# Spreading 1 / sum over a head's rows: products of 128 rows and 128 columns in place of 4 or 5 rows and 64 columns

## Chip, cores and metric

The kernel runs on one core of one Trainium2 chip. The metric is the device time of one execution in microseconds (us); of several executions the median counts.

## What is computed

Three stages follow each other, for a batch of 4 sequences of 576 tokens. The first is attention with 8 heads of 64 channels, in which each query row keeps only its 32 largest scores; the change stands here. The second is a gate (a causal convolution of 5 taps and a sigmoid) and two 512x512 products; the third mixes channels and tokens with cosines and sines.

```python
scores = scale * np.matmul(q, k.transpose(0, 1, 3, 2))
kth = np.partition(scores, -top_k, axis=-1)[..., -top_k:-top_k + 1]
scores = np.where(scores >= kth, scores, -1000000000.0)
scores = scores - np.max(scores, axis=-1, keepdims=True)
attn = np.exp(scores)
attn = attn / (np.sum(attn, axis=-1, keepdims=True) + 1e-09)
attn_out = np.matmul(attn, v)
...
x = gate(attn_out) * (attn_out @ w_val) @ w_out
...
theta = x @ w_theta
y = w_tok_r @ (x * cos(theta)) + w_tok_i @ (x * sin(theta))
u = x + y
out = u + np.maximum(u @ w_ch, 0.0)
```

## The kernel before

Attention works on pairs of heads (u, 16 of them), each cut into two **parts** by query tokens: x = 0 holds tokens 0 to 255, x = 1 holds tokens 256 to 575. There are 32 parts. A part is a run of tiles of 128 query rows by 576 keys: for each of the two heads (j) two tiles of 128 tokens (m), and in x = 1 one more tile that holds the last 64 tokens of both heads, one head's in its upper and the other's in its lower half. So a part has n = 4 or 5 tiles, and each has 128 sums of exponentials, one per partition.

The loop at the end of the kernel takes one tile a step, and in each step calls the pieces of several tiles in a written order (`STEP`, `SOON`): the score products (`scores_pe`, L536 and L537, into a PSUM bank for 256 keys and one for 320), their copy out by ScalarE (L550), the search for the 32nd largest value on VectorE and GpSimd (L572 to L599), the exponential (L193), mask and sum (L652), four transposes of the masked tile (L665) and one of its last 64 keys (L669), and the copies of these out (L684, L673). Between the steps `work` issues products of the later stages (L507, L805, L1107), so that TensorE has something to do while VectorE searches; that filling ends with the attention at about 736 us, and what is left of the last sequence runs alone.

Products that are small and need a little PSUM wait in the list `extras` and are put into the unused columns of a score bank: `scores_pe` issues the score products of 256 keys, then what fits beside them, then those of 320 keys, then what fits beside these. ScalarE copies both out later, in the order in which they were issued.

When a part's last tile is masked, `close` (a generator that the loop advances) does for it:

- L709 and L710: rs = 1 / (sums + 1e-9), 128 partitions by n columns, on GpSimd and VectorE.
- `rows` (L714, L717): TensorE transposes rs into n rows of 128, and ScalarE copies them into the SBUF tile rT.
- `columns(m)` for m = 0 and 1 (L731, L734, L738): TensorE spreads the row of head j over the 64 partitions of head j, and ScalarE copies the result into rb, 128 channels by 128 tokens (for m = 1 of x = 1 also the last 64 tokens). The stationary operand of such a product is one column of the identity matrix, read 64 times: with it, 64 output rows are each a copy of one row of rT.
- L758: the product of attention and v, px, in float32, two heads in two halves of the partitions.
- L776: VectorE multiplies px by rb into xT, which the gate and the next product read.

The two heads of `columns(m)` are two products: one writes PSUM partitions 0 to 63, the other 64 to 127. So each part has two **sets** of spreading products, 64 sets in all, and the first of a part (m = 0) stands behind L669, the second (m = 1) behind the score products of 320 keys. A float32 product shows as two MATMUL records in the trace (a transpose shows as one).

Of the kernel before, what the change touches and what calls it, by code (L numbers as in the profile page):

```python
# [11 lines left out]
F32 = mybir.dt.float32  # L12
# [78 lines left out]
def mixer(ctx, tc, qT, kT, vt, w_val, conv_t, w_out, w_theta, w_tok, w_ch, out, flag):  # L91
    nc = tc.nc
    safe = flag is None
    P = 128
# [20 lines left out]
    cp = ctx.enter_context(tc.tile_pool(name="cp", bufs=1))  # L115
    io = ctx.enter_context(tc.tile_pool(name="io", bufs=1))
    sp = ctx.enter_context(tc.tile_pool(name="sp", bufs=1))
    wk = ctx.enter_context(tc.tile_pool(name="wk", bufs=1))
# [44 lines left out]
    ident = cp.tile([P, P], F32, name="ident")  # L163
# [8 lines left out]
    nc.gpsimd.memset(trig_bias[64:], 0.0)  # L172
    half_pi = cp.tile([P, 1], F32, name="half_pi")
    nc.gpsimd.memset(half_pi, math.pi / 2)
    magic = cp.tile([P, 1], F32, name="magic")
    nc.gpsimd.memset(magic, MAGIC)

# [13 lines left out]
    def tabled(out, src, func, **more):  # L191

        ins = nc.scalar.activation(out, src, func, **more).ins  # L193
        table = func == AF.Sin
        if (not table) in last and TABLED:
            tc.add_manual_dep(ins, last[not table].name, mybir.DependencyInfo(
                mybir.DependencyClass.NoSync, mybir.DependencyReason.DATA), reason="one table at a time")
        last[table] = ins
# [489 lines left out]
    def diagonal(hp):  # L688

        if not diagonals:  # L690
            all_of = ml.tile([P, 2 * NC * ROOM[1]], F32, tag="room1", name="diagonals")
            diagonals["all"] = all_of[:, : NP * KW * P].rearrange("p (u k w) -> p u k w", u=NP, k=KW)
        if hp not in diagonals:
            diagonals[hp] = diagonals["all"][:, hp]
            nc.gpsimd.tensor_tensor(diagonals[hp], ident.unsqueeze(1).broadcast_to([P, KW, P]),
                                    W["conv"][:, hp, :].unsqueeze(2).broadcast_to([P, KW, P]), ALU.mult)
        return diagonals[hp]

    def close(part):

        u, x = part["u"], part["x"]
        b, hp = divmod(u, NP)
        lo, hi = COLS[x]
        w = hi - lo
        n = 4 + x
        rs = wk.tile([P, 5], F32, tag="rs", name=f"rs_{u}_{x}", bufs=2)
        rT = wk.tile([5, P], F32, tag="rT", name=f"rT_{u}_{x}")
        rb = wk.tile([P, S - CUT], F32, tag="rb", name=f"rb_{u}_{x}")
        nc.gpsimd.tensor_scalar(rs[:, :n], part["sums"][:, :n], 1e-9, None, ALU.add)  # L709
        nc.vector.reciprocal(rs[:, :n], rs[:, :n])  # L710
        done = set()

        def rows(spare):
            nc.tensor.transpose(spare[:n, :P], rs[:, :n], ident)  # L714

            def f():
                nc.scalar.copy(rT[:n], spare[:n, :P])  # L717
                done.add("rows")
            return f

        def row(k):
            return ident[:n, k : k + 1].broadcast_to([n, 64])

        def columns(m):


            def on_pe(spare):
                c = P + REM * (m * x)
                for j in range(2):
                    r = slice(64 * j, 64 * j + 64)  # L730
                    nc.tensor.matmul(spare[r, :P], row(2 * j + m), rT[:n], start=True, stop=True,  # L731
                                     skip_group_check=True)
                    if c > P:
                        nc.tensor.matmul(spare[r, P:c], row(4), rT[:n, r], start=True, stop=True,  # L734
                                         skip_group_check=True)

                def f():
                    nc.scalar.copy(rb[:, m * P : m * P + c], spare[:, :c])  # L738
                    done.add(m)
                return f  # L740
            return on_pe

        extras.append((P, rows))
        yield
        yield
        asked = "rows" in done
        if asked:
            extras.extend((P + REM * (x * m), columns(m)) for m in range(2))
        yield
        if x == 0:  # L750
            drain(("val", (u - 5) // NP))
        v, pT = part["v"], part["pT"]
        owed[0] -= 8.3 * w
        px = ps_m.tile([P, w], F32, tag="m", name=f"px_{u}_{x}")
        for c in range(NF + 1):
            for j in range(2):
                r, k = (slice(0, P), j * NF + c) if c < NF else (slice(REM * j, REM * j + REM), 2 * NF)
                nc.tensor.matmul(px[64 * j : 64 * j + 64, :], v[r, c, 64 * j : 64 * j + 64], pT[r, k, :],  # L758
                                 start=(c == 0), stop=(c == NF), skip_group_check=True)
        if x == 0:  # L760
            xt = sp.tile([P, PAD + S], F32, tag="xT", name=f"xT_{u}", bufs=5)
            nc.gpsimd.memset(xt[:, :PAD], 0.0)
            xT.setdefault(b, []).append(xt)
        xt = xT[b][hp]
        yield
        while "rows" not in done:
            yield
            yield
        if not asked:
            extras.extend((P + REM * (x * m), columns(m)) for m in range(2))  # L770
        yield
        yield
        while 1 not in done:
            yield
            yield
        nc.vector.tensor_tensor(xt[:, PAD + lo : PAD + hi], px, rb[:, :w], ALU.mult)  # L776
        there.add((u, x))
        split = b in SPLIT
        if not split and x == 0:
            return  # L780
        if split and x:
            g = gate[b][hp]
        else:
            drain(("gate", (u - GB) // NP))
            g = sp.tile([P, S], F32, tag="gp", name=f"gp_{u}", bufs=GB)
            gate.setdefault(b, []).append(g)
        if not split:
            lo = 0
        g = g[:, lo:hi]
        cw = W["conv"]  # L790
        if hp == NP - 1:
            jobs.append(front(b, (x,) if split else (0, 1)))
            if x:
                jobs.append(back(b))
        yield
        yield
        while lacking["conv"]:
            yield
            yield
        taps = [xt[:, k + lo : k + hi] for k in range(KW)]  # L800
        if split:
            owed[0] -= 1.675 * KW * (hi - lo)
            ps = ps_m.tile([P, hi - lo], F32, tag="m", name=f"pconv_{u}_{x}")
            for k in range(KW):
                nc.tensor.matmul(ps, diagonal(hp)[:, k, :], taps[k], start=(k == 0), stop=(k == KW - 1))  # L805
            yield
            yield
            tabled(g, ps, AF.Tanh, scale=0.5)
            ready.add((u, x))
            return  # L810
        nc.scalar.activation(g, taps[0], AF.Copy, scale=cw[:, hp, 0:1])
        for k in CT:
            ct = wk.tile([P, S], F32, tag="ct", name=f"ct_{u}_{x}_{k}")[:, : g.shape[1]]
            nc.scalar.activation(ct, taps[k], AF.Copy, scale=cw[:, hp, k : k + 1])
            nc.gpsimd.tensor_tensor(g, g, ct, ALU.add)
            yield
            yield
        if not CT:
            yield
            yield  # L820
        rest = [k for k in range(1, KW) if k not in CT]
        for k in rest:
            nc.vector.scalar_tensor_tensor(g, taps[k], cw[:, hp, k : k + 1], g, ALU.mult, ALU.add)
            if k == rest[1] and len(rest) > 2 or k == rest[-1]:
                yield
                yield
        tabled(g, g, AF.Tanh, scale=0.5)
        ready.add((u, x))
# [355 lines left out]
    for b in range(B):  # L1184
        late = b == B - 1
        f = 1.275 if b in THREE else 1.675
# [19 lines left out]
    def drain(key):  # L1206

        n = 0
        while key[1] >= 0 and key not in done:
            n += 1  # L1210
            assert n < 1000, (key, [(j.gi_frame.f_code.co_name, j.gi_frame.f_lineno, j.gi_frame.f_locals.get('b')) for j in jobs], sorted(map(str, done))[-40:], len(later), len(mid))
            run_mid()
            now, later[:] = list(later), []
            run(now)
            work(DRAIN)
# [24 lines left out]
    for k, part in enumerate(order):  # L1240
        i0 = part["tiles"][0].i
        u, x = part["u"], part["x"]
# [5 lines left out]
        elif split or x == 0:  # L1248
            when = (i0 - 7, i0 - 5, i0 - 5, i0 - 4, i0 - 3) if split or i0 and order[k - 1]["x"] and order[k - 1]["u"] // NP in SPLIT else (i0 - 9, i0 - 8, i0 - 7, i0 - 6, i0 - 3)
            a = (u, x if split else None)  # L1250
            for step, do in zip(when, (load_heads, split_high, split_low, *(
                    lambda u, x, j=j: double(u, j, x) for j in range(2)))):
# [37 lines left out]
    def begin_close(i):  # L1290
        e = seq[i]
        if e is e.part["tiles"][-1]:
            chains.append(close(e.part))
# [103 lines left out]
```

## Time and profile before

| | |
|---|---|
| median of 3 runs | 849.69 us (846.92 to 850.99) |
| the profiled execution, its own time | 849.38 us |
| its span, first to last instruction | 847.3 us |
| mean granted TensorE clock | 0.964 of full speed |
| TensorE busy | 754.7 us |
| VectorE busy | 679.4 us |
| ScalarE busy | 640.3 us |
| GpSimd busy | 438.5 us |

In the views, PE is TensorE's product and PEld its load of the stationary operand (the two overlap), DVE is VectorE, ACT ScalarE, POOL GpSimd, SP the queue of SyncE. L731 is line 731 of the kernel. "out<-in" names tiles; a shape such as 4*64 4x128 is a stationary operand of 4 rows and 64 columns and a moving operand of 4 rows and 128 columns. The chain of waits is followed back from the last instruction: at each step to what released it, or to the instruction before it on its engine; a piece of it lasts until the next piece begins. Time that an engine is idle and that "issue" ended is time in which it waited for no semaphore that the profile shows.

### The profile page before, as it was taken

To read this page: it belongs to the slowest core of one execution; us is meant where nothing else is said; L and a number is where in the kernel's file an instruction comes from. 1 tells how busy PE (TensorE), PEld (TensorE's weight loads), DVE (VectorE), ACT (ScalarE), POOL (GpSimd) and SP (SyncE) were. 2 spreads that over 40 slices of the span, in tenths; PEclk is the share of its full clock that TensorE was granted. 3 is DMA by queue.
4 is the path that set the end of the run, shared out by engine and by line. 5 is a ranking of instruction groups with operands and counts; after the bars stand their busy time and mean duration, and the time that the engine had idled before them with its cause. 6 is when DMAs were issued, how large, how long until landed. Compare 5 with 4: busy or idle time off the path is not lost.

```text
span 847.3 us, 16018 instructions
## 1 busy us (share of the span) xinstructions
PE 754.7 (89%) x4606; PEld 577.5 (68%) x4606; DVE 679.4 (80%) x2786; ACT 640.3 (76%) x1573; POOL 438.5 (52%) x575
## 2 busy tenths in 40 slices
PE   4478999969898899899699989999999899999995
PEld 3345667535655666677587666768897666798895
DVE  6999999879977888899889879989998686353521
ACT  6688898889778777889689887789987784336511
POOL 4876665545544545457667725537796143004600
PEclk9997799979999899999899999999999999999998
DMA  6566665634440243337455543234664300061002
GB/s 171 140 167 189 163 171 161 176 90 127 117 107 15 58 144 82 94 77 240 112 171 168 151 136 83 44 83 100 184 176 122 100 1 15 1 211 45 2 1 61
DMA packets 73602, 94.37 MB, mean 111 GB/s; under 512 B 13728, under 2 KB 37152, under 8 KB 73504
## 3 DMA queue, kind: packets, MB, share of 16 engines
q1 hardware_dynamic: 73184, 92.82, 40.3%
q8 instruction: 39, 0.64, 0.3%
q14 instruction: 59, 0.48, 0.2%
q10 hardware_dynamic: 320, 0.43, 0.2%
HBM read 49.96 MB, written 13.11 MB: 74 GB/s over the span
## 4 chain that ended last, share of the span: by engine, by line
PE 48%; DVE 27%; ACT 11%; POOL 6%; issue 4%; DMA 3%; SPq 1%; ACTq 0%; POOLq 0%
PE py L1107 8%; PE px L758 7%; DVE cand L572 6%; PE pval L507 5%; DVE thrs L599 4%; PE px2t L507 4%; PE pth L507 4%; PE ph L507 3%; PE pt L665 3%; DVE s L652 3%; PE py L1126 3%; PE ps L536 3%; POOL y L593 2%; DVE cand L578 2%; PE ps L537 2%
## 5 line engine op out<-in xcount | busy, mean ns | idle before, releaser
L593 POOL TENSOR_TENSOR y<-s,n 128x576 f32<-128x576 f32 x144 | 190.6, 1324 | 164.8 <-DVE thrs L599 118.6
L572 DVE MAX8 cand<-s 128x8 f32<-128x96 f32 x864 | 210.2, 244 | 1.4 <-ACT s L550 1.4
L652 DVE SCALAR_TENSOR_TENSOR s<-s,thrs,e 128x576 f32<-128x576 f32 x144 | 139.4, 968 | 9.7 <-ACT e L193 9.7
L585 ACT ACTIVATE n<-s,tops 128x576 bf16<-128x576 f32 x144 | 112.0, 778 | 39.6 <-POOL y L593 18.7
L550 ACT ACTIVATE s<-ps 128x256 f32<-128x256 f32 (+1 forms) x288 | 103.7, 406 | 32.9 <-PE ps L731 15.8
L665 PE MATMUL pt<-ident,s 128*128 128x128 f32 x576 | 96.2, 288 | 26.7 <-ACT pT L684 12.6
L1107 PE MATMUL py<-w_tok,z 128*128 128x256 f32 (+1 forms) x432 | 116.8, 410 | 3.4 <-DVE z L966 3.4
L599 DVE MAX8 thrs<-y 128x8 f32<-128x584 f32 x144 | 109.3, 759 | 6.8 <-POOL y L594 6.4
L758 PE MATMUL px<-pT,v 128*64 128x256 f32 (+3 forms) x640 | 106.7, 432 | 9.0 <-ACT pT L684 8.8
L193 ACT ACTIVATE e<-s,least 128x576 f32<-128x576 f32 x144 | 110.7, 769 | 0.5 <-DVE s L652 0.4
L665 PEld LDWEIGHTS pt<-ident,s 128*128 128x128 f32 x576 | 68.8, 145 | 55.6 <-ACT pT L684 22.4
L536 PE MATMUL ps<-kh_None,q 128*128 128x256 f32 x240 | 92.0, 390 | 4.1 <-ACT s L550 2.2
L684 ACT COPY pT<-pt 128x512 f32<-128x512 f32 x128 | 73.1, 571 | 28.5 <-PE pt L665 15.4
L1107 PEld LDWEIGHTS py<-w_tok,z 128*128 128x128 f32 x432 | 77.8, 191 | 24.0 <-DVE z L966 5.0
L758 PEld LDWEIGHTS px<-pT,v 128*64 128x64 f32 (+1 forms) x640 | 43.6, 140 | 57.6 <-issue 26.5
L576 DVE MAX8 tops<-cand 128x8 f32<-128x48 f32 x432 | 82.7, 191 | 0.1
L537 PE MATMUL ps<-kl_None,q 128*128 128x256 f32 x240 | 71.4, 300 | 0.0
L536 PEld LDWEIGHTS ps<-kh_None,q 128*128 128x128 f32 x240 | 46.4, 193 | 21.1 <-ACT s L550 6.1
L536 PE MATMUL ps<-kh,q 128*128 128x256 f32 (+1 forms) x80 | 37.5, 475 | 20.3 <-ACT s L550 8.6
L578 DVE MATCH_REPLACE8 cand<-tops,cand 128x48 f32<-128x48 f32 x288 | 55.1, 191 | 0.0
L673 ACT COPY pT<-ps 64x128 f32<-64x128 f32 (+1 forms) x160 | 39.3, 245 | 12.6 <-PE ps L669 5.8
L537 PEld LDWEIGHTS ps<-kl_None,q 128*128 128x128 f32 x240 | 47.0, 196 | 2.5 <-issue 0.9
(209 smaller groups left out, 1693.4 us busy)
## 6 DMA issues: line engine op xcount, KB each, us to landing
kh_None<-kh_None SPq DMA_DIRECT2D x48, 144.0 KB, 2.6
kl_None<-kl_None SPq DMA_DIRECT2D x48, 144.0 KB, 2.7
v<-in_vt_dram SPq DMA_DIRECT2D x20, 256.0 KB, 3.5
out_dram<-x2T SPq DMA_DIRECT2D x16, 256.0 KB, 3.2
w<-ch SPq DMA_DIRECT2D x16, 256.0 KB, 4.3
w<-theta SPq DMA_DIRECT2D x16, 256.0 KB, 5.4
raw_hi<-in_w_tok_dram SPq DMA_DIRECT2D x14, 256.0 KB, 4.1
kh<-kh SPq DMA_DIRECT2D x24, 144.0 KB, 2.6
```

The source lines that it names most:

```text
L193: ins = nc.scalar.activation(out, src, func, **more).ins
L507: nc.tensor.matmul(ps[o : o + n], x, y, start=(i + k == 0), stop=(i == last and k == len(ways) - 1), skip_group_check=(n < P))
L536: nc.tensor.matmul(bank[:, :w], q2, kh[:, lo:hi], start=(j == js[0]), stop=False)
L537: nc.tensor.matmul(bank[:, :w], q2, kl[:, lo:hi], start=False, stop=(j == js[-1]))
L572: nc.vector.max(d["cand"][:, k, 8 * x : 8 * x + 8], s_tiles[i][:, x * SUB : (x + 1) * SUB])
L585: nc.scalar.activation(n, s_tiles[i], AF.Sign, bias=d["tops"][:, k, KC - 1 : KC], scale=-(1.0 + 2.0 ** -22), accum_out=acc)
L593: nc.gpsimd.tensor_tensor(y[:, :S], s_tiles[i], d.pop(("n", k)), ALU.mult)
L599: nc.vector.max(thrs[:, N - 1 - i : N - 1 - i + NK], d.pop(("y", k)))
L652: nc.vector.scalar_tensor_tensor(p, p, thr(i), e.exp, ALU.is_ge, ALU.mult, accum_out=part["sums"][:, e.slot : e.slot + 1])
L665: nc.tensor.transpose(e.pt[:, c, :], p[:, c * P : (c + 1) * P], ident)
L758: nc.tensor.matmul(px[64 * j : 64 * j + 64, :], v[r, c, 64 * j : 64 * j + 64], pT[r, k, :], start=(c == 0), stop=(c == NF), skip_group_che ...
L1107: nc.tensor.matmul(ps, z[:, m * P : (m + 1) * P], W["tok"][:, w, lo:hi], start=(i + k == 0), stop=(i == NF))
```

## The change

Seven setup instructions on GpSimd are added per copy of the program (the second copy, for unusual inputs, is not run): `spread` holds six blocks of 64 columns and a seventh, filled with identity columns 0, 2, 1, 3, nothing, 4, nothing. Two neighbouring blocks make one constant of 128 rows and 128 columns: it copies one row of rT to output partitions 0 to 63 and another to 64 to 127. `rT` becomes one tile of 128 rows, cleared once, of which each part overwrites the first n. `columns(m)` then issues one product for both heads; for the last 64 tokens it issues two, which are added in PSUM, each with one zero block.

```diff
@@ setup @@
     half_pi = cp.tile([P, 1], F32, name="half_pi")
     nc.gpsimd.memset(half_pi, math.pi / 2)
+    spread = cp.tile([P, 7, 64], F32, name="spread")
+    nc.gpsimd.memset(spread, 0.0)
+    for i, k in enumerate((0, 2, 1, 3, None, 4)):
+        if k is not None:
+            nc.gpsimd.tensor_copy(spread[:, i, :], ident[:, k : k + 1].broadcast_to([P, 64]))
+    rT = cp.tile([P, P], F32, name="rT")
+    nc.gpsimd.memset(rT, 0.0)
@@ close @@
         rs = wk.tile([P, 5], F32, tag="rs", name=f"rs_{u}_{x}", bufs=2)
-        rT = wk.tile([5, P], F32, tag="rT", name=f"rT_{u}_{x}")
...
-        def row(k):
-            return ident[:n, k : k + 1].broadcast_to([n, 64])
+        def rows_of(i):
+            return spread[:, i : i + 2, :].rearrange("p a w -> p (a w)")
...
                 c = P + REM * (m * x)
-                for j in range(2):
-                    r = slice(64 * j, 64 * j + 64)
-                    nc.tensor.matmul(spare[r, :P], row(2 * j + m), rT[:n], start=True, stop=True,
-                                     skip_group_check=True)
-                    if c > P:
-                        nc.tensor.matmul(spare[r, P:c], row(4), rT[:n, r], start=True, stop=True,
-                                         skip_group_check=True)
+                nc.tensor.matmul(spare[:, :P], rows_of(2 * m), rT, start=True, stop=True,
+                                 skip_group_check=True)
+                for j in range(2 if c > P else 0):
+                    nc.tensor.matmul(spare[:, P:c], rows_of(5 - j), rT[:, 64 * j : 64 * j + 64],
+                                     start=(j == 0), stop=(j == 1), skip_group_check=True)
```

What stands on TensorE in the step of a part with x = 1, before the change (ps is the score bank, kh and kl the keys in two halves, s the masked tile whose last keys L669 transposes):

```order
L537 MATMUL ps_0_1869<-kl_3_1_1738,q_87 128x256
L669 MATMUL ps_0_1869<-ident,s_1270 64x128
L731 MATMUL ps_0_1869<-rT_1_1695,ident 64x128 x2
L536 MATMUL ps_256_1875<-kh_3_1_1737,q_87 128x320
L537 MATMUL ps_256_1875<-kl_3_1_1738,q_87 128x320
L731 MATMUL ps_256_1875<-rT_1_1695,ident 64x128
L734 MATMUL ps_256_1875<-rT_1_1695,ident 64x64
L731 MATMUL ps_256_1875<-rT_1_1695,ident 64x128
L734 MATMUL ps_256_1875<-rT_1_1695,ident 64x64
L665 MATMUL pt_1917<-ident,s_1325 128x128 x4
```

The same step with the change, in which lines stand 7 further down:

```order
L676 MATMUL ps_0_1865<-ident,s_1272 64x128
L735 MATMUL ps_0_1865<-rT,spread 128x128
L543 MATMUL ps_256_1870<-kh_3_1_1733,q_87 128x320
L544 MATMUL ps_256_1870<-kl_3_1_1734,q_87 128x320
L735 MATMUL ps_256_1870<-rT,spread 128x128
L738 MATMUL ps_256_1870<-rT,spread 128x64 x2
L672 MATMUL pt_1911<-ident,s_1325 128x128 x4
```

The new products stand in the places of the old ones. A part with x = 0 has the same step without the products of 64 columns (L734 before, L738 now). The order on VectorE, ScalarE and SyncE is the same in both programs; on TensorE beside this a handful of neighbouring products change places, and on GpSimd the setup grows.

## Rows read from the trace of the kernel before

**Rows 1.** The page: TensorE's busy time; shares of the chain of waits by engine.
```profile
PE 754.7 (89%) x4606; PEld 577.5 (68%) x4606; DVE 679.4 (80%) x2786; ACT 640.3 (76%) x1573; POOL 438.5 (52%) x575
...
PE 48%; DVE 27%; ACT 11%; POOL 6%; issue 4%; DMA 3%; SPq 1%; ACTq 0%; POOLq 0%
```

**Rows 2.** Stretches: us, busy PE, PEld, DVE, ACT, POOL, granted clock, DMA share, GB/s.
```profile
60.00:100.00 40.00, 32.81 (x172) 22.24 (x171) 39.69 (x177) 33.98 (x93) 25.26 (x38) 0.80 0.71 190
...
512.00:562.00 50.00, 50.00 (x294) 36.36 (x290) 44.59 (x208) 38.13 (x95) 25.65 (x34) 1.00 0.35 83
```

**Rows 3.** Records that read rT: duration min/median/max in ns, first and last start.
```profile
L731 PE MATMUL ps<-rT,ident x256: 267/292/472, 61.3 to 735.4; 4*64 4x128 f32 x64, 5*64 5x128 f32 x64
...
L734 PE MATMUL ps<-rT,ident x64: 214/216/217, 139.8 to 735.6; 5*64 5x64 f32 x64
```

**Rows 4.** Chain of waits, 517 to 521.3 us: start us, us, what.
```profile
517.29 0.11 PE ps L669
517.40 0.36 PE ps L731 x4
517.76 0.35 PE ps L536
518.11 0.15 PE ps L537
518.25 0.36 PE ps L731 x4
518.62 0.59 PE pt L665 x4
...
520.74 0.11 PE ps L669
520.84 0.11 PE ps L714
520.95 0.15 PE ps L536
521.10 0.15 PE ps L537
```

**Rows 5.** Waits of TensorE's weight loads: us in total, times, longest us.
```profile
PEld px L758 <- issue: 26.5, 81, 1.0
...
PEld ps L731 <- issue: 11.7, 59, 0.3
```

**Rows 6.** Chain of waits, 137.9 to 141 us: a second set of x = 1.
```profile
139.59 0.37 PE ps L731 x4
139.96 0.12 PE ps L734 x4
140.07 0.59 PE pt L665 x4
```

**Rows 7.** Chain of waits, 691.5 to 703.5 us: two sets back to back.
```profile
692.35 0.58 PE ps L731 x8
692.93 0.20 PE ps L714
693.13 0.44 PE pt L665 x4
...
702.12 0.63 PE ps L731 x8
702.75 0.12 PE ps L734 x2
```

**Rows 8.** Chain of waits: the first and the last set that lies on it.
```profile
97.70 0.62 PE ps L731 x4
...
735.05 0.63 PE ps L731 x8
```

**Rows 9.** Timeline of GpSimd around the end of the setup.
```profile
1.95 0.30 POOL masks.py:199 TENSOR_SCALAR_AFFINE_SELECT ident<-ident 128x128 f32<-128x128 f32 x1
12.44 0.73 POOL L291 TENSOR_TENSOR q<-raw,q 64x256 fp32r<-64x256 f32 x1 [10.18 <-ACT q L289]
```

## The prediction

> **What bounds the kernel now.** I read the page first. TensorE is busy 89% of the span, and the chain that ended last lies 48% on it and 27% on VectorE [rows 1]. So no engine bounds the whole: what a change on TensorE is worth depends on the stretch. The stretches show it [rows 2]: between 60 and 100 us VectorE is busy 39.69 of 40 us and TensorE 32.81, so there VectorE sets the pace; between 512 and 562 us TensorE is busy all 50 us and VectorE 44.59. The reader is to see that TensorE time is worth its full price in stretches of the second kind, and something between nothing and that in the first.
>
> Then I read the lines that the diff touches. L731 has 256 records, four for each of the 64 sets, and L734 has 64, in the 16 second sets of x = 1 [rows 3]. Their busy time is small; what they cost is in the chain, where one step with a set and one without stand three microseconds apart [rows 4]. Without a set, L669, L714, L536 and L537 follow each other by 0.11, 0.11, 0.15 and 0.15 us. With a set, L669 is again 0.11, but L731 holds the chain for 0.36, the L536 behind it for 0.35 instead of 0.15, and the L665 behind the second set for 0.59 instead of the 0.44 that four transposes take behind other transposes or L714 [rows 7]. Weight loads show where it goes [rows 5]: before L731 the load is idle 11.7 us in 59 times, 0.20 us each, with no semaphore to wait for, and before L758 26.5 us in 81 times. L714 is no entry of that kind, though it too reads what another engine has just made, and writes a few columns of the same bank. What L731 and L758 share and L714, L669 and L536 don't is that they write one half of the output partitions each. I conclude that TensorE empties itself when it goes from whole products to halves, and again when it goes back.
>
> The Trainium skill says the same ("TensorEngine Tiling (Array Packing)", Key Properties): changing the tiling mode, not just the tile, drains the engine. The trace agrees as far as it goes: 0.20 us at the way in [rows 5], and at the way out 0.35 against 0.15 [rows 4].
>
> The four records of a set take 0.36 us of chain with some 0.15 to 0.2 of idle in it, though single-file records take 0.11 each, or 0.44 for four. So the two halves run side by side. That is what the change gives up.
>
> **The change part by part.**
>
> *First sets (m = 0).* The new form is one product of whole rows and columns, two records of 128 columns. The trace has no float32 product of just that shape; nearest are L714 and L669, 0.11 us a record [rows 4], so 0.22. The set and the L536 behind it go from 0.36 + 0.35 to 0.22 + 0.15: **0.34 us less**. If emptying stayed, it would be 0 (0.36 + 0.35 again, since a pair side by side takes as long as one whole product); that is the low end.
>
> *Second sets of x = 0.* From 0.36 + 0.59 [rows 4] to 0.22 + 0.44 [rows 7]: **0.29 us less**.
>
> *Second sets of x = 1.* Before, L731, L734 and L665 hold 0.37 + 0.12 + 0.59 = 1.08 us [rows 6]. Now there is the product of 0.22, and two of 64 moving columns for the last tokens, four records. Each streams half as many columns as L714's but must load a stationary operand of 128 columns, which the trace never shows apart from a 128-column stream: between 0.05 (half of 0.11) and 0.11 us, so 0.22 to 0.44 together. With 0.44 for L665 it makes 0.88 to 1.10 us: 0.20 less to 0.02 more. I take **0**, near the upper end, since the only transposes with a stationary operand of 128 columns here, L665's, take 0.11 each.
>
> *The four last parts* have no score products left, and their two sets stand back to back. At 692 us the sets and L714 hold 0.58 + 0.20 [rows 7]; four records and L714 make 5 x 0.11 = 0.55: 0.23 less, twice. At 702 us it is 0.63 + 0.12 + 0.59 [rows 7, 6] against 8 x 0.11 + 0.44 = 1.32: 0.02 less, twice. Together **0.5 us**.
>
> *Setup.* Seven small instructions on GpSimd, none larger than the 0.30 us of the selection in the identity, so at most 2.1 us. GpSimd is idle 10.18 us right behind that selection, until ScalarE has made q [rows 9], and the first use is at 61 us [rows 3]. Nothing is on the path; without that cover it would be 2.1 us, once.
>
> *The rest.* rT was one buffer before and is one now, so ScalarE's copy into it waits for the same readers as before. ScalarE copies the same shapes to rb. The order of VectorE, ScalarE and SyncE is unchanged. Sets get shorter for those who wait behind them as well: ScalarE copies the scores out when the bank's last product is done.
>
> **The sum.** Following the chain through the trace, 32 of the 64 sets lie on it, the first at 97.70 us and the last at 735.05 us [rows 8]; at the others the chain is on another engine or a transfer. The 32 are 12 first sets, 8 second sets of x = 0, 4 second sets of x = 1, and the 8 of the last four parts: 12 x 0.34 + 8 x 0.29 + 0 + 0.5 = 4.1 + 2.3 + 0.5 = **6.9 us**. The profiled execution took 849.4 us (its span is 847.3), 0.3 under the median of 849.7, so the sum gives 842.5.
>
> **The rivals.**
>
> *Every set counts.* The chain is one path of many, and a wait for VectorE is often a wait for scores that TensorE gave late. All sets: 28 x 0.34 + 14 x 0.29 + 0.5 = 14.1 us, 835.3 us; with the low price for the last columns (14 x 0.2 + 0.4 = 3.2 more) 832. For it: TensorE holds 48% of the chain [rows 1]. Against it: between 60 and 100 us VectorE is idle 0.3 of 40 us [rows 2], so it can hardly be served sooner.
>
> *The time is freed and waits again.* The freed time goes into the next wait for VectorE or ScalarE, except where TensorE alone sets the pace: 512 to 562 us [rows 2] with 3 first sets and 2 second sets of x = 0, and the last four parts. That leaves 3 x 0.34 + 2 x 0.29 + 0.5 = 2.1 us: 847.3. For it: outside such stretches the engines are busy to similar shares [rows 1]. Against: the chain already leaves out the stretches where others lead.
>
> *Emptying stays, pairs are lost (slower).* If the idle time belongs to something that the new form keeps, such as reading rT just after ScalarE wrote it, then the sets gain nothing, and the products for the last 64 tokens, which ran side by side, go in single file. Before they add 0.13 us to a set (0.37 + 0.12 against 0.36) [rows 4, 6], now 0.22 to 0.44: 0.09 to 0.31 more. With 6 on the chain that is 0.5 to 1.9 us, with all 16 up to 5: 850 to 854.4, likeliest 851. It decides if the weight load behind L669 still starts 0.3 us late. Against it: L714, which reads rs just written, starts 0.11 behind L669 [rows 4].
>
> The Trainium skill has the rule that this rival rests on ("TensorE: Matmul & The Clock Gate", Part 3): products of fewer than 128 columns, put into different column groups, run at the same time, so it recommends the form that is taken out here. The trace shows that they do run side by side; by that rule alone the change could only lose, some 851 us.
>
> *The clock.* It is granted at 0.80 of full speed between 60 and 100 us [rows 2], so part of the stretch ran at the lower of the two levels. Whether whole products and less idle time move such falls, the trace can't say; either sign, a few us, and it widens the range.
>
> **How the numbers follow.** About 0.5% (4.2 us) is what a measurement of this kernel can tell from no change. The chain's sum, 839 to 845, has 0.53; every set counts, 832 to 839, 0.2; freed time waits again, 845 to 849, 0.22; slower than before 0.05, of which little passes 854. Faster by over 0.5% (under 845.4) is the first two and a bit of the third: 0.76; within 0.5% 0.21; slower 0.03. The range of 8 in 10 runs from 835 to 847.5.
>
> **What would show it right or wrong.** Right: behind L669 the new product starts within 0.12 us, with no idle weight load that "issue" ended; it holds the chain for 0.22, and the L536 behind it for about 0.15. The last-column products are two pairs of records, 0.05 to 0.11 each. The waits of L758 stay at 26 us, since its halves stay. The time from 736 us to the end stays as it is and only moves forward. Wrong: if these steps shrink so and the end does not move by 4 us or more, then the chain overstated TensorE, and waits for VectorE's s, cand or thrs have grown in its place. If the steps do not shrink, halves were not the reason for the idle time. If the time falls by over 12 us, the sets off the chain counted.

## The result, and the profile after

The median went from 849.61 us to 840.25 us (4 executions each): ratio 0.9895, 95% interval 0.9869 to 0.9921. Measured again later, beside two further kernels and more executions of before, the ratio was 0.9916 (0.9902 to 0.9931). By the two ratios the change takes 7 to 9 us off; 842.5 had been forecast, in a range of 835 to 847.5.

The page of the changed kernel, to be held against [rows 1]: busy time by engine, and the shares of the chain of waits.

```profile
PE 737.7 (88%) x4478; PEld 581.3 (69%) x4478; DVE 677.9 (81%) x2786; ACT 639.6 (76%) x1573; POOL 441.4 (53%) x582
...
PE 39%; DVE 28%; ACT 15%; POOL 6%; issue 5%; DMA 4%; SPq 1%; ACTq 0%; POOLq 0%
```

TensorE lost 128 records, and its share of the chain fell from 48% to 39%; ScalarE took 4 of the 9 points. Lines stand 4, 6 or 7 further down than before: L731 is L735, L734 is L738, L758 is L762; L710 is L716, L714 is L720; L669 is L676, L536 is L543, L537 is L544, L665 is L672.

The records that read rT in the changed kernel (columns as in [rows 3]): 128 and 64, with stationary operands of 128 rows and columns.

```profile
L735 PE MATMUL ps<-rT,spread x128: 270/273/275, 61.0 to 726.7; 128*128 128x128 f32 x128
...
L738 PE MATMUL ps<-rT,spread x64: 222/275/275, 139.6 to 727.1; 128*128 128x64 f32 x64
```

The chain of the changed kernel from 512.8 to 517.5 us, the same step as in [rows 4] (start us, us, what):

```profile
513.17 0.11 PE ps L676
513.28 0.22 PE ps L735 x2
513.51 0.15 PE ps L543
513.65 0.14 PE ps L544
513.80 0.22 PE ps L735 x2
514.02 0.44 PE pt L672 x4
```

A set holds the chain for 0.22 us where it held it for 0.36, the product behind the first set for 0.15 where it was 0.35, the four transposes behind the second for 0.44 where they were 0.59. That is what had been worked out, to the hundredth.

The chain of the changed kernel at a second set of x = 1, from 646 to 648 us:

```profile
646.82 0.22 PE ps L735 x2
647.04 0.39 PE ps L738 x4
647.43 0.44 PE pt L672 x4
```

Together 1.05 us, against 1.08 before [rows 6]: 0.03 less. A record of the last tokens takes 0.10 us, though it streams half as many columns as the one ahead of it. Two of the four last parts, in the chain from 684 to 697 us:

```profile
684.29 0.45 PE ps L735 x4
684.73 0.11 PE ps L720
...
693.83 0.45 PE ps L735 x4
694.28 0.39 PE ps L738 x4
694.67 0.44 PE pt L672 x4
```

0.56 against 0.78, and 1.28 against 1.34 [rows 7, 6]: 0.22 and 0.06 less, where 0.23 and 0.02 had been forecast. And the waits of TensorE's weight loads, to be held against [rows 5]:

```profile
PEld pt L672 <- ACT pT L691: 26.4, 21, 6.6
PEld px L762 <- issue: 26.0, 80, 0.5
PEld ps L543 <- ACT s L557: 23.5, 35, 2.3
...
PEld pth L514 <- issue: 6.2, 24, 0.5
```

The 11.7 us of idle loads before the spreading products are gone from the list, and those of L762, which still writes halves, stay. What grew are the waits for ScalarE: for pT 22.4 us before, for s 18.9. A part of the freed time waits there. GpSimd's longer setup went where it was expected (its timeline, changed kernel):

```profile
1.66 0.48 POOL L176 MEMSET spread<- 128x448 f32 x1
...
2.55 0.95 POOL L179 COPY spread<-ident 128x64 f32<-128x64 f32 x5
...
12.30 0.74 POOL L298 TENSOR_TENSOR q<-raw,q 64x256 fp32r<-64x256 f32 x1 [8.59 <-ACT q L296]
```

It ends at 3.5 us, and 8.6 us of the idle time of [rows 9] are left behind it. One of the seven instructions, the clearing of spread, takes 0.48 us, where none had been put over 0.30; with the idle time behind it that costs nothing.

Where the time was gained is read from one instruction of each part, the reciprocal of VectorE (L710 before, L716 after). The table says by how many us it starts sooner than in the trace of before (a minus: later), worked out from the starts in both traces; after_again is a second trace of the changed kernel, and the last two columns belong to experiments below.

| part, start before (us) | changed kernel | after_again | on_chain | off_chain |
|---|---|---|---|---|
| 1st, 49.4 | 0.1 | 0.2 | 0.2 | 0.2 |
| 4th, 101.6 | -0.9 | -0.9 | 0.6 | -0.9 |
| 8th, 200.5 | 0.2 | 0.2 | 1.7 | 0.1 |
| 12th, 294.8 | 0.9 | 0.9 | 3.1 | 0.3 |
| 16th, 377.8 | 3.0 | 2.9 | 3.7 | 0.7 |
| 20th, 465.9 | 4.1 | 4.1 | 4.1 | 0.7 |
| 24th, 552.2 | 5.0 | 5.1 | 5.1 | 0.8 |
| 28th, 634.6 | 7.1 | 6.5 | 4.8 | 1.3 |
| 32nd, 721.3 | 8.3 | 7.8 | 7.2 | 1.3 |

Up to 200 us nothing is gained, and at the 4th part the changed kernel is even 0.9 us late. Then it wins about a microsecond for every two or four parts, and next to nothing more from 736 us to the end (the span is 8.5 us shorter).

### The profile page after: what moved, and what is told of

Same layout as the page of the kernel before. It is cut to its first block, busy times and chain, and to the rows that moved or that the text cites. A ratio compares the mean times of both kernels' runs of the same rounds, so it can differ in the third digit from the quotient of the medians.

```text
span 838.8 us, 15738 instructions
## 1 busy us (share of the span) xinstructions
PE 737.7 (88%) x4478; PEld 581.3 (69%) x4478; DVE 677.9 (81%) x2786; ACT 639.6 (76%) x1573; POOL 441.4 (53%) x582
## 4 chain that ended last, share of the span: by engine, by line
PE 39%; DVE 28%; ACT 15%; POOL 6%; issue 5%; DMA 4%; SPq 1%; ACTq 0%; POOLq 0%
PE py L1111 7%; DVE cand L579 6%; PE px L762 6%; DVE thrs L606 4%; PE pth L514 4%; PE ph L514 3%; DVE s L659 3%; PE px2t L514 3%; PE pval L514 3%; PE py L1130 3%; ACT n L592 3%; PE pt L672 3%; DVE cand L585 2%; ACT e L200 2%; DVE tops L583 2%
## 5 line engine op out<-in xcount | busy, mean ns | idle before, releaser
L659 DVE SCALAR_TENSOR_TENSOR s<-s,thrs,e 128x576 f32<-128x576 f32 x144 | 137.2, 953 | 9.7 <-ACT e L200 9.7
L672 PE MATMUL pt<-ident,s 128*128 128x128 f32 x576 | 95.3, 287 | 29.5 <-ACT pT L691 16.6
L762 PE MATMUL px<-pT,v 128*64 128x256 f32 (+3 forms) x640 | 104.2, 425 | 10.3 <-ACT pT L691 10.3
L672 PEld LDWEIGHTS pt<-ident,s 128*128 128x128 f32 x576 | 69.5, 146 | 56.9 <-ACT pT L691 26.4
L543 PE MATMUL ps<-kh_None,q 128*128 128x256 f32 x240 | 91.2, 387 | 5.0 <-ACT s L557 2.5
L762 PEld LDWEIGHTS px<-pT,v 128*64 128x64 f32 (+1 forms) x640 | 43.1, 137 | 57.0 <-issue 26.0
L544 PE MATMUL ps<-kl_None,q 128*128 128x256 f32 x240 | 71.2, 300 | 0.0
L543 PEld LDWEIGHTS ps<-kh_None,q 128*128 128x128 f32 x240 | 46.3, 193 | 19.4 <-ACT s L557 7.7
L543 PE MATMUL ps<-kh,q 128*128 128x256 f32 (+1 forms) x80 | 35.5, 451 | 22.9 <-ACT s L557 10.0
L544 PEld LDWEIGHTS ps<-kl_None,q 128*128 128x128 f32 x240 | 46.7, 195 | 2.3 <-issue 0.9
```

What stands on the lines that cost most here:

```text
L543: nc.tensor.matmul(bank[:, :w], q2, kh[:, lo:hi], start=(j == js[0]), stop=False)
L544: nc.tensor.matmul(bank[:, :w], q2, kl[:, lo:hi], start=False, stop=(j == js[-1]))
L659: nc.vector.scalar_tensor_tensor(p, p, thr(i), e.exp, ALU.is_ge, ALU.mult, accum_out=part["sums"][:, e.slot : e.slot + 1])
L672: nc.tensor.transpose(e.pt[:, c, :], p[:, c * P : (c + 1) * P], ident)
```

## Experiments

Two questions were open. The prediction took it that TensorE empties itself between products of all output partitions and products of one half. The old form was narrow in two ways, though, few rows and half the columns, and the trace of before had shown neither alone. And it took it that only the sets on the chain count.

**Rows or columns.** few_rows keeps the change's 128 columns, with 4 or 5 rows:

```diff
-                nc.tensor.matmul(spare[:, :P], rows_of(2 * m), rT, start=True, stop=True,
+                nc.tensor.matmul(spare[:, :P], rows_of(2 * m)[:n], rT[:n], start=True, stop=True,
...
-                    nc.tensor.matmul(spare[:, P:c], rows_of(5 - j), rT[:, 64 * j : 64 * j + 64],
+                    nc.tensor.matmul(spare[:, P:c], rows_of(5 - j)[:n], rT[:n, 64 * j : 64 * j + 64],
```

> The change's products of 128 columns, but with only the 4 or 5 rows that carry data (rows of spread and of rT cut to n). Theory A, TensorE empties itself between products that write all output partitions and products that write one half of them: no idle weight load before the spreading products, first sets hold the chain for 0.22 us as after the change, time 840 us (838 to 842). Rival B, it empties because only 4 or 5 of 128 rows are used: the idle 0.20 us before the set and the 0.20 us behind it are back, 847 to 850 us.

halves keeps all 128 rows, with two products of 64 columns:

```diff
-                nc.tensor.matmul(spare[:, :P], rows_of(2 * m), rT, start=True, stop=True,
-                                 skip_group_check=True)
...
+                for j in range(2):
+                    r = slice(64 * j, 64 * j + 64)
+                    nc.tensor.matmul(spare[r, :P], spread[:, 2 * m + j, :], rT, start=True, stop=True,
+                                     skip_group_check=True)
+                    if c > P:
+                        nc.tensor.matmul(spare[r, P:c], spread[:, 5, :], rT[:, r], start=True, stop=True,
+                                         skip_group_check=True)
```

> All 128 rows of the constant and of rT, but the two heads as two products of 64 columns again, also for the last 64 tokens: rows new, columns as before the change. Theory A: the idle time of 0.20 us on both sides of a set is back and the pairs run side by side, 848 to 851 us. Rival B (few rows are the cause): 838 to 842 us, with no idle weight load.

few_rows: 851.9 us, ratio to before 1.0049 (1.0031 to 1.0068). halves: 848.93 us, 1.001 (0.9999 to 1.0021). Neither keeps any of the gain. Both theories had named one cause and each kernel keeps one; both bring the idle time back. halves came in where theory A had put it (848 to 851); few_rows lies above both of its forecasts. The chain of few_rows from 518.97 us, then the idle weight loads of the same kernel:

```profile
518.97 0.41 PE ps L735 x2
519.38 0.35 PE ps L543
519.73 0.14 PE ps L544
519.87 0.41 PE ps L735 x2
520.29 0.59 PE pt L672 x4
```

```profile
PEld ps L735 <- issue: 11.7, 59, 0.3
```

The chain of halves from 517.95 us, and its idle weight loads:

```profile
517.95 0.37 PE ps L737 x4
518.32 0.35 PE ps L543
```

```profile
PEld ps L737 <- issue: 11.8, 59, 0.4
```

The reader is to see 0.35 behind the set in both, as in [rows 4], and 11.7 and 11.8 us of idle loads in 59 times, as in [rows 5]. So few rows alone empty TensorE, and halves alone do too. A narrow shape by itself is not enough, though. L676 has 128 rows and 64 columns and stands between whole products without an idle load, in this kernel too, and the load of L737, of the same 128 rows and 64 columns, is idle right behind it. The weight loads of halves from 517.5 us:

```profile
517.57 0.11 PEld L676 LDWEIGHTS ps<-ident,s 128*64 128x64 f32 x1
517.87 0.20 PEld L737 LDWEIGHTS ps<-rT,spread 128*64 128x64 f32 x4 [0.19 <-issue]
518.24 0.19 PEld L543 LDWEIGHTS ps<-kh_None,q 128*128 128x128 f32 x1 [0.17 <-issue]
```

L676 is a transpose and writes the first half of the partitions alone; the first product of L737 writes the same half, is no transpose, and has a partner in the other half. Which of the two decides, no run here separates.

few_rows is even slower than before, since it gives up the halves' running side by side as well (0.41 for a set against 0.36) and keeps the idle time. That is the cost of the prediction's slower rival, met in a kernel (it had been priced at 850 to 854.4), though not the cause that the rival named.

**The idle time put back.** forced leaves the change as it is and puts a product of 64 by 4 columns ahead of each whole one:

```diff
+                nc.tensor.matmul(spare[64:, :4], spread[:, 2 * m, :], rT[:, :4], start=True, stop=True,
+                                 skip_group_check=True)
                 nc.tensor.matmul(spare[:, :P], rows_of(2 * m), rT, start=True, stop=True,
```

> The change, and ahead of each whole product a small one of 64 columns by 4 that writes PSUM partitions 64 to 127 and is overwritten at once: 128 records more (64 products of two records) of at most 0.06 us each. Theory A: each of the 64 sets gets both idle times back, so first sets cost 0.3 us more and second sets, x = 1 included, 0.3 us more: 849 to 853 us. Rival C, the gain came from fewer and wider records and from ScalarE getting its bank sooner, not from emptying: 128 records of at most 0.06 us on a path that holds half of them, 841 to 844 us.

856.29 us, ratio to before 1.0094 (1.0069 to 1.0118), some 1.8 to 2% over the changed kernel. Its chain from 521.93 us, where L735 is the small product and L737 the whole one:

```profile
521.93 0.11 PE ps L676
522.04 0.21 PE ps L735 x2
522.25 0.42 PE ps L737 x2
522.67 0.15 PE ps L543
```

A set holds the chain for 0.63 us in place of 0.22, 0.41 more: 0.21 is the small product with the way in, and 0.20 the whole product behind it, which takes 0.42 in place of 0.22. How much of the 0.21 the small product would take without the way in, the trace doesn't show. 64 sets by 0.41 are 26 us, of which 15 to 17 reach the end. I had expected 849 to 853; a set costs 0.1 us more than the 0.3 I had put down. The rival that the gain came from fewer records or from ScalarE's earlier bank falls: 841 to 844 us was its time.

**Which sets count.** on_chain has the change in the 16 parts whose sets lay on the chain of before, off_chain in the other 16; the rest of each keeps the old products.

```diff
+ON_CHAIN = {(2, 0), (0, 1), (4, 0), (6, 0), (8, 0), (10, 0), (10, 1), (11, 0), (12, 0), (12, 1),
+            (13, 0), (13, 1), (14, 0), (14, 1), (15, 0), (15, 1)}
...
+                if (u, x) in ON_CHAIN:
...
+                else:
```

> The change in the 16 parts alone whose sets lay on the chain of waits before, the old products in the other 16. By the prediction's step (only sets on the chain count) the whole gain is here: 9.4 us, 840 us against 849 of before. By the rival that every freed piece of TensorE time counts alike (9.4 us gained of 14.1 freed): 6.9 us are freed here, two thirds of that is 4.6, so 844.5 us.

> The complement: the change in the 16 parts whose sets lay off the chain, the old products in the others. By the prediction's step nothing is gained: 848 to 850 us. By the rival that every freed piece counts alike: 7.2 us freed, two thirds 4.8, so 844 us.

on_chain: 841.97 us, ratio 0.9926 (0.9911 to 0.9941), 6.3 us gained, 5.0 to 7.5. off_chain: 847.85 us, ratio 0.9993 (0.9983 to 1.0002), 0.6 us, and it can't be told from nothing. About as much TensorE time is freed in both (6.9 and 7.2 us, by the prediction's prices; its busy time falls by 6.6 and 9.8 us), so the chain was right in telling them apart. The expected times were not met as closely: on_chain lies between the 840 of the chain and the 844.5 of the rival, and its 6.3 us are fewer than the 9.4 that had been counted on; off_chain lies at the lower end of the chain's 848 to 850 and far from the rival's 844. The two gains add up to 6.9 us; the changed kernel has 7.1 in one measurement and 8.9 in the other, so whether the sets off the chain bring up to two us more once the others are shorter stays open. The clock doesn't account for the gain: on_chain was granted 0.961 to 0.965 and before, beside it, 0.956 to 0.967, and off_chain had 0.960 to 0.969 with the time of before.

**Without the transposes.** After the change the transpose of rs and its copy serve only to turn 1 / sum into rows. direct drops both: ScalarE copies each column of rs 64 times into a stationary operand, the identity moves, and the last tokens need one product.

```diff
-                nc.tensor.matmul(spare[:, :P], rows_of(2 * m), rT, start=True, stop=True,
+                nc.tensor.matmul(spare[:, :P], rows_of(m), ident, start=True, stop=True,
                                  skip_group_check=True)
...
+                if c > P:
+                    nc.tensor.matmul(spare[:, P:c], rows_of(2), stack, start=True, stop=True,
+                                     skip_group_check=True)
...
+        nc.scalar.copy(wide[:, :n], rs[:, :n].unsqueeze(2).broadcast_to([P, n, 64]))
```

Here rows_of(i) is two neighbouring blocks of wide, and stack the two halves of the identity's columns added up. So that neighbouring blocks belong to the two heads, the sums are stored in another order; in x = 1 the column of the last tile is taken twice, each time with the other head's half made next to zero.

> No transpose and no rT: ScalarE copies the columns of rs, each 64 times, into a stationary operand of 128 rows, and the identity is the moving operand; for the last 64 tokens one product, two records, in place of four. TensorE loses 32 records of 0.11 us (transposes) and 16 x 0.2 us of the 0.39 us that the last tokens take after the change, 6.7 us in all; ScalarE copies 128x256 or 128x384 in place of 4x128 or 5x128, 0.1 to 0.3 us more in each of 32 parts. If TensorE time counts as it did in the change (9.4 us of the 14 us freed), 836 us (834 to 838). If ScalarE's copies stand on the path, 840 to 843 us.

845.44 us, ratio 0.9972 (0.9953 to 0.9992): slower than the change, and above both expected ranges (834 to 838, and 840 to 843). It has 64 TensorE records fewer than the change (4414), though TensorE's busy time isn't lower (742.1 us against 737.7). But the products are asked for some steps sooner in it, and the order on the engines is another one. expand puts ScalarE's copy where that of rT stood:

```diff
+        def rows(spare):
+            def f():
+                nc.scalar.copy(wide[:, :n], rs[:, :n].unsqueeze(2).broadcast_to([P, n, 64]))
+                done.add("rows")
+            return f
...
-        nc.scalar.copy(wide[:, :n], rs[:, :n].unsqueeze(2).broadcast_to([P, n, 64]))
+        extras.append((P, rows))
```

> As direct, but ScalarE's copy of rs into the stationary operand stands where its copy of rT stood, so that the order of VectorE and ScalarE is that of the change. TensorE loses 32 transposes of 0.11 us and 16 x 0.2 us for the last tokens; ScalarE's copy is 0.13 to 0.27 us longer in each of 32 parts. If the order was what made direct slow: 836 to 839 us. If ScalarE's longer copies stand on the path: 841 to 846 us, as direct.

839.27 us, ratio 0.9885 (0.9869 to 0.9901), 0.3 us above the 836 to 839 that were expected if the order was the cause. The two kernels differ only in where that copy stands and in when the products are asked for, so the order was what made direct slow, not ScalarE's longer copies. How expand stands to the change, 0.9895 or 0.9916, that measurement doesn't settle.

**The next change of shape.** L762 goes through three shapes. Its weight loads in the changed kernel (timeline, 689 to 693 us; the idle time before each in brackets):

```profile
689.21 1.81 PEld L762 LDWEIGHTS px<-pT,v 128*64 128x64 f32 x16 [0.33 <-DVE s L659]
691.51 0.19 PEld L762 LDWEIGHTS px<-pT,v 64*64 64x64 f32 x4 [0.49 <-issue]
692.20 0.42 PEld L672 LDWEIGHTS pt<-ident,s 128*128 128x128 f32 x4 [0.49 <-issue]
```

px_whole makes the last shape whole, with v's two blocks on the diagonal of a tile that is zero elsewhere; px_expand is that and expand.

```diff
-        for c in range(NF + 1):
+        for c in range(NF):
             for j in range(2):
...
+        nc.tensor.matmul(px, v[:, NF, :], pT[:, 2 * NF, :], start=False, stop=True, skip_group_check=True)
```

> The changed kernel as it is, beside the next two on one chip: 840 us, ratio 0.989 to before.

> The change, and in the product of attention and v the last 64 keys of both heads as one product of 128 rows and 128 columns (v's two blocks on the diagonal, zeros beside them) in place of two of 64 rows and 64 columns. After the change such a product goes from whole to 128x64 halves, to 64x64 quarters and back: the quarters' weight load is idle 0.49 us behind the halves. If each change of shape empties TensorE, one of three is gone, 0.15 us of 32 parts, 4.8 us freed, two thirds of it 3.2: 837 us, ratio 0.985 to 0.987. If halves and quarters follow each other without emptying, 840 us.

> The edits of px_whole and of expand together. If both free time on TensorE that counts for two thirds: 835 to 837 us. If expand's longer copies on ScalarE give it back, no faster than px_whole.

On one chip: the change 841.42 us, ratio 0.9916 (0.9902 to 0.9931); px_whole 839.0, 0.9887 (0.9873 to 0.9902); px_expand 836.87, 0.9861 (0.9847 to 0.9876). The change came out 1.4 us over the 840 expected, px_whole 2 over its 837, and px_expand in its 835 to 837. px_whole's interval just touches that of the change, so that it is faster is likely, not shown; that of px_expand lies clear of it, 4.6 us by the medians, and is the fastest of all. The chain of the changed kernel, then of px_whole, at the product at 689 us:

```profile
689.28 2.99 PE px L762 x20
692.27 0.59 PE pt L672 x4
```

```profile
689.49 2.31 PE px L763 x16
691.80 0.74 PE px L765 x2
692.53 0.44 PE pt L674 x4
```

3.58 us became 3.49: the idle time on the way out is gone (0.44 for the transposes), and the whole product pays some of it back, 0.74 for two records. So 0.09 us are freed here where 0.15 had been put down, 3 us in 32 parts, and some 2.4 were measured by the medians.

## Why the prediction was right

- **What the emptying costs.** Right, and in size too: 0.34 and 0.29 us for sets were forecast, and the chain of the changed kernel gives the same differences. The price came from one step that stood beside its own control, a step with L714 in the place of a set.
- **Why it empties.** The step "what L731 and L758 share is that they write one half of the output partitions each" was half of it. L731 was narrow in rows as well, and few_rows shows that this alone has the same price. Nor did the step fit every row: it counts L669 among the products that don't write one half, yet L669 writes 64 partitions (64x128 in the order listed above) and no load before it is idle, as L676 in halves shows again. L714, by the prediction no entry of that kind, has two such loads of 32, 0.3 us in all. The rule on the tiling mode that the prediction quotes (the Trainium skill, "TensorEngine Tiling (Array Packing)", Key Properties) speaks of the mode, rows and columns alike; by that rule few_rows and halves both had to lose the gain, and the runs agree: 1.0049 and 1.001. In which mode L676 runs, and so why its 64 columns cost nothing, no run here shows.
- **Last tokens.** 0 was taken between 0.20 less and 0.02 more; 0.03 less was measured.
- **The sum.** 6.9 us for the sets on the chain; on_chain measured 6.3 (5.0 to 7.5). The forecast of 842.5 stands 0.3% over the first measurement and 0.1% over the second.
- **What it missed.** The sets at 97.7 and 99.7 us and those at 138.7 and 139.6 lay on the chain [rows 8, 6], some 1 us of the sum, and the changed kernel had won 0.2 us by 200 us. That is no scatter, since its second trace shows the same to 0.1 us. on_chain, with fewer sets changed, had won 1.7 by then, and off_chain no more than the full change, so changing the early sets off the chain seems to cost something there; why stays open. Later the changed kernel gained more than the chain said: 7.4 us from the 12th to the 32nd part (6.9 in the second trace), where the sets on the chain make up some 5. The two misses go opposite ways, so that the total came out so near is in part luck.
- **The rivals.** "Every set counts" falls with off_chain. "Freed and waits again" (847.3) falls with the time; what is true of it are the 4 and 4.6 us by which the waits for ScalarE's pT and s grew. "Emptying stays, pairs are lost" was the slower side; few_rows has its cost. The rule that it rests on (the Trainium skill, "TensorE: Matmul & The Clock Gate", Part 3) holds as far as the halves' running side by side goes (four records of the last tokens held 0.12 us [rows 6], in single file 0.39), and says nothing of the way in and out, which costs more here than a pair saves.

## What to carry to other kernels

Look for weight loads that are idle for a few tenths of a microsecond with no semaphore to wait for. Before the change those of L731, and 70 of the 81 of L758, stood where the form of the product changes (whole, halves, quarters or few rows). It is a hint, not a proof: of the 24 of L514 in the changed kernel's list 16 stand between two whole products of 512 columns, 0.24 us each. A step with the product beside one without it gives the price, as in [rows 4]. A few narrow products among whole ones are better padded to 128 rows and 128 columns with zeros, as long as the padded stream is not much longer than the narrow ones side by side. When an engine's time is freed all over a program, the chain of waits tells rather well which part of it counts; change those places alone and the others alone to see it.

## What the runs showed of the hardware

- 4 or 5 rows at all 128 columns cost the same idle time as two halves of 64 columns (11.7 and 11.8 us in 59 times), so being narrow in one direction is enough. It is not always so: transposes of 128 rows with 64 columns (L676) or with 4 or 5 (L720), which write from the first partition on, hold the chain for 0.11 us among whole products.
- Leaving whole products for a tiny one of 64 by 4 columns and coming back costs 0.41 us a time, the tiny product included, and 15 to 17 us in this kernel.
- A record with a stationary operand of 128 columns takes 0.10 us of the chain even when only 64 columns stream.
- direct and expand do the same work, and direct only asks for the products some steps sooner: 845.44 against 839.27 us. Such a place in the written order was worth nearly as much as the change itself.
